# Folding a softmax into the first weight matrix with seven block products instead of eight, on a kernel bound by TensorE

## The chip, the cores and the metric

The kernel runs on one core of a Trainium2 chip. The metric is the device time of one execution in microseconds. Before the change it is 718.34 us, the median of 9 runs that lie between 718.19 and 718.52 us. A change of about 0.2% (1.4 us) is the least that a measurement here can tell from none.

## What is computed

The inputs are `q`, `k`, `v` of shape (4, 6080, 256), and two weight matrices `w_in` (256 x 2048) and `w_out` (2048 x 256), all fp32.

```python
# per batch b
qn = q / (norm(q, axis=1) + 1e-6);  kn = k / (norm(k, axis=1) + 1e-6)
a  = softmax(kn.T @ qn / tau)               # 256 x 256
x  = v @ a                                  # 6080 x 256
# over all 4 x 6080 tokens
g  = s * relu(x @ w_in) ** 2 + b
out = g @ w_out
```

The kernel never forms `x`. It folds the softmax into the weights: `v @ (a @ w_in)`, so that each batch has a folded matrix `wa = a @ w_in` (256 x 2048).

## The kernel before, in words

**Tiles and groups.** The tokens are taken in 48 groups of 512 (the last has 256). A group is worked in 16 steps, one for each 128 columns of `wa`. In step `m`, `mm1` (L661) makes two matmuls of 512 columns into one half of a PSUM tile `h_ps`; after two steps ScalarE takes the whole tile through a relu (L671). `h_ps` has two buffers. The squares of the relus are made on ScalarE after steps 3 and 5 (L682) and on VectorE after steps 8, 12 and 0 of the next group (L684).

**The second product, with seven.** For groups 1 to 46 `g @ w_out` is made by a Strassen-like scheme of seven block products in place of eight (`seven_items`, L829): 112 matmuls of 128 columns for a group, 7 in each step of the next group, one product finished every 16 matmuls. Its sums of `g` are made on VectorE (`sums_of`, after steps 2, 3, 6 and 10), and after each product VectorE scales it out of PSUM (`evacuate`, L689; called u or o_sb by what it writes).

**The order is written by hand.** The main loop runs over the steps. In each step it issues `mm1`, then any `early` function, then seven matmuls of the second product, then the relu, the squares and the sums, and at last the functions that stand for this step in `side`. `po` keeps the program order on each engine. So where a function stands in the step decides what is ahead of it in the queue of its engine.

**Batches.** While the groups of batch b are worked, the Gram matrix and the norms of batch b+1 are made on the side. Near the end of batch b `finish_ops` (placed by `fin_step` through the table `FIN`) takes the norms to inverse norms, scales, takes exponentials (`eT`, L302), sums their rows (L312) and their reciprocals (`rs`, L317), and then folds: `fold_one` makes a block of `wa`, 512 columns for one half m of the rows, from two matmuls of 512 columns that accumulate in PSUM (L329), and `scaled` writes it as fp16 times `rs`, on ScalarE for m = 0 (L322) and on VectorE for m = 1 (L324). For batches 1 to 3 there are 8 such blocks, three steps apart. All of them use one PSUM bank, the only buffer of the pool `ps_gram`, so a fold's first matmul waits until the block before it has been read. `wa` has two buffers (`apool`).

**The start.** Batch 0 has nothing to hide behind. Its last three chunks of `q` and `k` (one of four rows a partition, two of two) are treated alone: their squares are made as they land (L177, L171, L174), the first chunk's squares are folded once from four rows to two on VectorE (`half`, L222), for k and for q, and matmuls with a vector of ones sum them (`add_norms`, L246 for k, L250 for q). Then come the inverse norms (L271), the scaling (L296), the exponentials, a first folded block of 256 columns (`first_block`, L345), two more folds of the second 256 columns (`folds[:2]`, L329), and only then the main loop. The other folds of batch 0 stand in `early`, by the table `FOLDS`.

```python
FIN = (0, 3, 5, 7, 9, 11, 13, 17, 19, 22)
FOLDS = (1, 1, 3, 3, 5, 5, 8, 8)
for f in (first_block, *folds[:2]):
    f()
```

Of the kernel before, what the change touches and what calls it, by code (L numbers as in the profile page):

```python
# [9 lines left out]
FP16 = mybir.dt.float16  # L10
# [3 lines left out]
ALU = mybir.AluOpType  # L14
# [3 lines left out]
def kernel(  # L18
# [47 lines left out]
    wpool = pool("wpool", 1)  # L66
    qk_pool = pool("qk_pool", 8)
    sq_pool = pool("sq_pool", 2)
    late_pool = pool("late_pool", NLATE)
    f3_pool = pool("f3_pool", 13)  # L70
    sm_pool = pool("sm", 1)
    apool = pool("apool", 2)
# [3 lines left out]
    gpool = pool("gpool", 2)  # L76
    spool = pool("spool", 1)
    upool = pool("upool", 4)
    opool = pool("opool", 2)

    ps_gram = pool("ps_gram", 1, space=PSUM)
# [29 lines left out]
    class Gram:  # L111
# [45 lines left out]
        def norm_ops(self, c):  # L157

            qc, kc = self.tiles[c]
            _, np_, jc = self.chunks[c]  # L160
            st = {}

            at_end = self.b == 0 and c >= len(self.chunks) - NLATE

            def squares(a, js):
                def f():
                    if "sq" not in st:
                        st["sq"] = (late_pool if at_end else sq_pool).tile(
                            [P, 2, JC, C], FP16, tag="sq", name="sq")
# [12 lines left out]
            def fold(half, arrays, last):  # L182
                def f():
                    src = st["f", 2 * half] if 2 * half < jc else st["sq"]
                    if ("f", half) not in st:
                        if last:
                            t = f3_pool.tile([P, 2, 1, C], FP16, tag="f3", name="f3")
                        else:
                            t = sq_pool.tile([P, 2, half, C], FP16, tag=f"f{half}", name="f")
                        st["f", half] = t  # L190
                    po(nc.vector.tensor_add(  # L191
                        st["f", half][:np_, arrays], src[:np_, arrays, :half, :],
                        src[:np_, arrays, half : 2 * half, :]))
                    if last and c == 0:
                        self.first = st["f", half]
                    if last and (c == 0 or self.b > 0 and c == len(self.chunks) - 1):
                        for rows in self.rows:
                            rows.append((st["f", half], np_, 1))
                return f

            def into_first():

                dst, src = self.first[:np_], st["f", 1][:np_]
                if self.b == 0:
                    po(nc.vector.tensor_add(dst, dst, src))
# [10 lines left out]
            if at_end and jc == 2:  # L216
                return ops + [unfolded]
            if at_end:
                def half(a):
                    if "h" not in st:  # L220
                        st["h"] = sq_pool.tile([P, 2, 2, C], FP16, tag="f2", name="h")
                    po(nc.vector.tensor_add(st["h"][:np_, a], st["sq"][:np_, a, :2],  # L222
                                            st["sq"][:np_, a, 2:]))
                    self.rows[a].append((st["h"], np_, 2))
                return ops + [half]
            if jc == 8:
                ops += [fold(4, slice(0, 1), False), fold(4, slice(1, 2), False)]
            ops += [fold(2, slice(0, 2), False), fold(1, slice(0, 2), True)]
            return ops + [into_first] if 0 < c < len(self.chunks) - 1 else ops
# [24 lines left out]
        def finish_ops(self):  # L254
# [3 lines left out]
            def inverse(a=None):  # L258

                n = C + CH if a is None else (CH, C)[a]  # L260

                def part(i):
                    if i == 0:
                        st["r", a] = sm_pool.tile([P, n], FP32, tag=f"r{a}", name=f"r{a}")
                        if a is None:
                            st["r", 1], st["r", 0] = st["r", a][:, :C], st["r", a][:, C:]
                    r = st["r", a]
                    func, kw = [(AF.Ln, dict(bias=tiny)), (AF.Exp, dict(scale=0.5)),
                                (AF.Ln, dict(bias=eps)), (AF.Exp, dict(scale=-1.0))][i]
# [84 lines left out]
            def fold_one(f0, n, m):  # L354
                def f():
                    wa_ps = self.bank("wa_ps", CH, C).rearrange("p a c -> p (a c)")[:, :n]
                    fold_mm(f0, n, m, wa_ps)
                    scaled(f0, n, m, wa_ps)
                return f

            if self.b == 0:
                blocks = [(2 * P, 2 * P), (4 * P, 2 * P), (6 * P, 2 * P), (2 * NW, NW), (3 * NW, NW)]
            else:
                blocks = [(f0, NW) for f0 in range(0, Dff, NW)]
            folds = [fold_one(f0, n, m) for f0, n in blocks for m in range(CH)]
            if self.b == 0:
                return [norms(1), *inverse(1), norms(0), *inverse(0), lambda: scale(CH),
                        lambda: first_block(2 * P)] + folds
            return [copy_out, norms_both, *inverse(), scale, lambda: exps(0), lambda: exps(1),
                    sums] + folds  # L370

        def bank(self, name, a, b):

# [144 lines left out]
        f()  # L518
    transpose_v(0)
    keep_busy(1)  # L520
    for f in (first_block, *folds[:2]):
        f()


    acc = opool.tile([P, 4, C], FP32, tag="o_sb", name="acc")
# [38 lines left out]
        po(nc.scalar.copy(out=T[:, ts(i, 2), :], in_=w[:, 0, :, :P] if T is T2 else w[:, 0, :, P:]))  # L564


    side, early = {}, {}

    def at_step(s, f):
# [2 lines left out]

    FIN = (0, 3, 5, 7, 9, 11, 13, 17, 19, 22)
    first_group = [b * N // TG for b in range(B)]
    FOLDS = (1, 1, 3, 3, 5, 5, 8, 8)
    for i, f in enumerate(folds[2:]):
        early.setdefault(FOLDS[i], []).append(f)
    at_step(14, lambda: po(nc.vector.tensor_scalar_mul(
        out=s_out, in0=s_bc, scalar1=1.0 / (LAM * LAM))))
# [22 lines left out]
    for b in range(1, B):  # L602
        gr = grams[b]
        w0 = first_group[b - 1] * FT + (26 if b == 1 else 6)
        w1 = first_group[b] * FT - 3
        NCH = len(gr.chunks)
        fin_len = 54
        span = (w1 - fin_len) - w0 - 12
        n = NCH * JC
        for c in range(NCH):  # L610
            sc = w0 + span * c * JC / n
            at_step(max(3, sc - 16), lambda gr=gr, c=c: gr.load(c))
            if c == 0:
                at_step(sc, gr.start)
            for j in range(JC):
                at_step(w0 + span * (c * JC + j) / n, lambda gr=gr, c=c, j=j: gr.mm(c, j))

            def norm_step(gr=gr, c=c, sc=sc):
                ops = gr.norm_ops(c)
                for i, f in enumerate(ops):  # L620
                    at_step(int(sc) + 2 + 1 + i * 3, f)
            at_step(sc + 1, norm_step)

        def fin_step(gr=gr, s=w1 - fin_len):
            ops = gr.finish_ops()
            for i, f in enumerate(ops):
                at_step(int(s) + 1 + (FIN[i] if i < len(FIN) else FIN[-1] + 3 * (i - len(FIN) + 1)), f)
        at_step(w1 - fin_len - 12, fin_step)


# [292 lines left out]
```

## Time and profile before

| | |
|---|---|
| median of 9 runs | 718.34 us |
| the profiled execution | 718.34 us, of which the trace's span is 716.6 us |
| PE (TensorE) busy | 697.1 us, 7417 matmuls |
| VectorE (DVE) busy | 624.4 us, 878 instructions |
| ScalarE (ACT) busy | 544.8 us, 592 instructions |
| granted TensorE clock | 0.997 |
| fold matmuls (L329, 512 columns) | 56 |
| fold results scaled on ACT (L322, 512 columns) | 13, mean 683 ns |
| fold results scaled on DVE (L324, 512 columns) | 15, mean 744 ns |

The profiled execution took exactly the median, and 1.7 us of it lie outside the span. A busy PE means that matmuls follow one another; their recorded durations overlap, so durations are better read from start to start. In the lines of the trace a name like `wa_ps<-w_in,eT` says what an instruction writes and reads, `L329` is its line in the code, and a bracket at the end tells how long the engine was idle and which instruction ended it.

### The profile page before, as it was taken

The page shows a single profiled execution, that of the slowest core. Times are in us where ns is not written, and L with a number is a line of the kernel's source. Part 1 is how long each engine was busy: PE and PEld are TensorE (multiplying, and loading weights), DVE is VectorE, ACT ScalarE, POOL GpSimd, SP SyncE. Part 2 cuts the span into 40 slices and gives each one's busy share as a digit, 9 for nine tenths or more (in the row PEclk, how much of TensorE's full clock was granted, in tenths as well). Part 3 has the DMA queues.
Part 4 walks back from the last instruction along what each step waited for, and adds up shares of the span by engine and source line. Part 5 has one row for each costly group of instructions (what it writes and reads, how often), then busy time and mean ns, then how long its engine had stood idle before and what let it go on. Part 6 is the DMA issues. An engine that isn't in the chain of part 4 may idle for free.

```text
span 716.6 us, 17483 instructions
## 1 busy us (share of the span) xinstructions
PE 697.1 (97%) x7417; PEld 503.7 (70%) x7417; DVE 624.4 (87%) x878; ACT 544.8 (76%) x592; POOL 110.9 (15%) x189
## 2 busy tenths in 40 slices
PE   4699999999999999999999999999999999999998
PEld 2456777776677777777677777777668777777777
DVE  4889999988789989998889899998887888888886
ACT  5779877787777777778777778777877777777875
POOL 4532332102101222101010222110000000000000
PEclk9999999999999999999999999999999999999999
DMA  9999999635565978444663878943323333321202
GB/s 236 207 259 170 156 176 140 120 91 121 113 124 109 136 134 144 112 89 94 135 143 59 147 132 126 153 91 75 100 63 75 94 71 75 97 60 46 82 31 75
DMA packets 87454, 83.47 MB, mean 116 GB/s; under 512 B 56304, under 2 KB 62256, under 8 KB 87376
## 3 DMA queue, kind: packets, MB, share of 16 engines
q0 software_dynamic: 26608, 43.40, 38.3%
q1 hardware_dynamic: 60192, 37.64, 21.8%
q8 instruction: 58, 0.95, 0.6%
q10 hardware_dynamic: 576, 1.31, 0.5%
q14 instruction: 20, 0.16, 0.1%
HBM read 78.91 MB, written 24.90 MB: 145 GB/s over the span
## 4 chain that ended last, share of the span: by engine, by line
PE 92%; DMA 4%; DVE 2%; ACT 1%; issue 0%; DVEq 0%; ACTq 0%
PE h_ps L661 45%; PE o_ps L829 40%; PE s_ps L148 4%; PE wa_ps L329 2%; DMA qk<-in_k_dram 1%; DMA raw<-in_q_dram 1%; DMA w_in<-in_moe_w_in_dram 1%; PE o_ps L733 1%; ACT sq L177 1%; DVE f L191 1%; PE o_ps L707 0%; ACT r L671 0%; DVE sq L174 0%; DVE o_sb L689 0%; DVE S L758 0%
## 5 line engine op out<-in xcount | busy, mean ns | idle before, releaser
L671 ACT ACTIVATE r<-h_ps 128x1024 f16<-128x1024 f32 (+1 forms) x384 | 388.4, 1014 | 152.3 <-PE h_ps L661 147.6
L661 PE MATMUL h_ps<-vT,wa 128*128 128x512 f16 (+7 forms) x1632 | 452.1, 364 | 0.1
L829 PEld LDWEIGHTS <-S 128*128 128x128 f16 x2944 | 198.0, 98 | 84.8 <-issue 0.2
L829 PEld LDWEIGHTS <-g 128*128 128x128 f16 x2208 | 155.1, 98 | 74.1
L684 DVE TENSOR_TENSOR g<-r 128x2048 f16<-128x2048 f16 (+2 forms) x150 | 174.7, 1165 | 14.0 <-ACT r L671 13.4
L829 PE MATMUL o_ps<-T,S 128*128 128x128 f16 x2208 | 183.3, 219 | 0.1
L661 PEld LDWEIGHTS <-wa 128*128 128x128 f16 x1632 | 136.0, 98 | 20.1 <-DVE wa L324 0.5
L829 PE MATMUL o_ps<-w_out,g 128*128 128x128 f16 x1472 | 134.3, 219 | 0.2 <-DVE u L689 0.2
L689 DVE SCALAR_TENSOR_TENSOR o_sb<-o_ps,s_out,u 128x256 f32<-128x256 f32 x138 | 66.5, 482 | 50.8 <-PE o_ps L829 48.7
L682 ACT ACTIVATE g<-r 128x1024 f16<-128x1024 f16 (+1 forms) x97 | 100.4, 1035 | 0.2
L148 PE MATMUL s_ps<-qk 128*128 128x256 f16 (+1 forms) x384 | 72.0, 290 | 13.5 <-ACT qk L139 9.0
L388 POOL DMA_DIRECT2D v<-in_v_dram x48 | 30.9, 648 | 264.8 <-DMA vT<-v 209.7
L689 DVE SCALAR_TENSOR_TENSOR u<-o_ps,s_out,rowconst 128x256 f32<-128x256 f32 x138 | 65.8, 477 | 0.0
L829 PE MATMUL o_ps<-w_out,S 128*128 128x128 f16 x736 | 63.5, 219 | 0.0
L829 PE MATMUL o_ps<-N,g 128*128 128x128 f16 x736 | 63.4, 219 | 0.0
L207 POOL DMA_DIRECT2D f<-f x30 | 26.3, 876 | 223.8 <-DVE f L191 187.4
L758 DVE TENSOR_TENSOR S<-S,g 128x2048 f16<-128x2048 f16 (+1 forms) x47 | 56.4, 1201 | 1.3
L177 ACT ACTIVATE sq<-qk 128x1024 f16<-128x1024 f16 (+2 forms) x53 | 54.5, 1041 | 3.9 <-DMA qk<-in_k_dram 2.2
L756 DVE TENSOR_TENSOR S<-g 128x2048 f16<-128x2048 f16 (+1 forms) x47 | 56.1, 1193 | 0.0
L762 DVE TENSOR_TENSOR S<-g,S 128x2048 f16<-128x2048 f16 x46 | 55.9, 1216 | 0.0
L760 DVE TENSOR_TENSOR S<-g 128x2048 f16<-128x2048 f16 x46 | 55.9, 1215 | 0.0
L148 PEld LDWEIGHTS <-qk 128*128 128x128 f16 (+1 forms) x384 | 33.1, 104 | 20.5 <-ACT qk L139 9.5
(85 smaller groups left out, 314.0 us busy)
## 6 DMA issues: line engine op xcount, KB each, us to landing
out_dram<-o_sb SPq DMA_DIRECT2D x42, 512.0 KB, 2.9
v<-in_v_dram POOLq DMA_DIRECT2D x47, 256.0 KB, 4.9
qk<-in_k_dram POOLq DMA_DIRECT2D x42, 256.0 KB, 6.8
qk<-in_q_dram POOLq DMA_DIRECT2D x42, 256.0 KB, 7.6
f<-f POOLq DMA_DIRECT2D x30, 128.0 KB, 3.1
vT<-v SPq DMA_TRANSPOSE x182, 3.0
out_dram<-o_sb SPq DMA_DIRECT2D x10, 256.0 KB, 4.1
w<-in_moe_w_out_dram POOLq DMA_DIRECT2D x4, 512.0 KB, 10.1
```

The source lines that it names most:

```text
L148: po(nc.tensor.matmul(self.s_ps[:, ch, :], qc[:np_, j, ts(ch, P)], kc[:np_, j, :], start=(c == 0 and j == 0 and ch == 0), stop=(c == len(s ...
L177: po(nc.scalar.activation(out=st["sq"][:np_, a, js, :], in_=(qc, kc)[a][:np_, js, :], func=AF.Square))
L661: po(nc.tensor.matmul(dst, wa[:, ci, ts(m, P)], src, start=(ci == 0), stop=(ci == CH - 1), skip_group_check=True))
L671: po(nc.scalar.activation(out=r16[:, :, i % 2, :n], in_=h_tiles.pop((g, i))[:, :, :n], func=AF.Relu))
L682: po(nc.scalar.activation(out=dst, in_=src, func=AF.Square))
L684: po(nc.vector.tensor_mul(dst, src, src))
L689: po(nc.vector.scalar_tensor_tensor(out=dst, in0=src, scalar=s_out, op0=ALU.mult, in1=add, op1=ALU.add))
L756: po(nc.vector.tensor_add(T[1], A21, A22))
L758: po(nc.vector.tensor_sub(T[2], T[1], A11))
L760: po(nc.vector.tensor_sub(T[3], A11, A21))
L762: po(nc.vector.tensor_sub(T[4], A12, T[2]))
L829: po(nc.tensor.matmul(st[name][:, j, :], a()[:, i, ts(j, P)], w[:, i, :], start=first, stop=last, skip_group_check=True))
```

## The change

There are three parts.

1. **Start.** The two folds of the second 256 columns are no longer made ahead of the main loop, but in its step 0, after the first two `mm1` matmuls.
2. **Start.** Of the first of the last three chunks, only the squares of k are folded from four rows to two. The rows of q's squares are summed as they are: 8 small matmuls in place of a VectorE addition and 4.
3. **Folds of batches 1 to 3.** The 8 blocks of two matmuls are replaced by seven products for each half of the columns, 14 matmuls of 512 columns in all. They need sums of the halves of `eT` (`half_sums`, four VectorE operations of 128 columns for a batch) and of the halves of `w_in` (`w_in_sums`, four VectorE operations of 1024 columns, once, kept in the buffers of the last chunks' squares). Partial results are accumulated on in the same bank: after each product the bank is read, and the next product is added to what stands there (`new` marks the three of seven that begin afresh). Three of seven readings are kept as fp32 (`keep`, ScalarE), one goes to `wa` by ScalarE and three by VectorE with a kept one added (`out`). The products stand 2.4 steps apart, rounded down, in place of 3.

The diff, cut to its core:

```diff
-    late_pool = pool("late_pool", NLATE)
+    late_pool = pool("late_pool", 1)
+    fold_pool = pool("fold_pool", 1)
...
             if at_end:
-                def half(a):
-                    if "h" not in st:
-                        st["h"] = sq_pool.tile([P, 2, 2, C], FP16, tag="f2", name="h")
-                    po(nc.vector.tensor_add(st["h"][:np_, a], st["sq"][:np_, a, :2],
-                                            st["sq"][:np_, a, 2:]))
-                    self.rows[a].append((st["h"], np_, 2))
-                return ops + [half]
+                def rows(a):
+                    if a == 0 or jc == 2:
+                        return unfolded(a)
+                    half = sq_pool.tile([P, 2, 2, C], FP16, tag="f2", name="half")
+                    po(nc.vector.tensor_add(half[:np_, 1], st["sq"][:np_, 1, :2], st["sq"][:np_, 1, 2:]))
+                    self.rows[1].append((half, np_, 2))
+                return ops + [rows]
...
+            def half_sums():
+                A = lambda m, k: st["e"][:, k, ts(m, P)]
+                S = st["S"] = [fold_pool.tile([P, P], FP16, tag=f"S{n}", name=f"S{n}")
+                               for n in range(1, 5)]
+                po(nc.vector.tensor_add(S[0], A(1, 0), A(1, 1)))
+                po(nc.vector.tensor_sub(S[1], S[0], A(0, 0)))
+                po(nc.vector.tensor_sub(S[2], A(0, 0), A(1, 0)))
+                po(nc.vector.tensor_sub(S[3], A(0, 1), S[1]))
+
+            def seven_folds(p):
+                A = lambda m, k: st["e"][:, k, ts(m, P)]
+                B = lambda k, n: w_in16[:, k, ds(n * (Dff // 2) + p * NW, NW)]
+                T = lambda n: W[n][:, ts(p, NW)]
+                S = lambda n: st["S"][n - 1]
+                C_ = lambda m, n: self.wa[:, m, ds(n * (Dff // 2) + p * NW, NW)]
+                rs = lambda m: st["rs"][:, m : m + 1]
+                u = {}
+                def product(a, w, then, new=False):
+                    def f():
+                        if new:
+                            st["wa_ps"] = self.bank("wa_ps", CH, C).rearrange("p a c -> p (a c)")
+                        po(nc.tensor.matmul(st["wa_ps"], a(), w(), start=new, stop=True,
+                                            skip_group_check=True))
+                        then()
+                    return f
+                def keep(n, m):
+                    def f():
+                        u[n] = fold_pool.tile([P, NW], FP32, tag=f"u{n}", name=f"u{n}")
+                        po(nc.scalar.mul(out=u[n], in_=st["wa_ps"], mul=rs(m)))
+                    return f
+                def out(m, n, k=None):
+                    def f():
+                        if k is None:
+                            po(nc.scalar.mul(out=C_(m, n), in_=st["wa_ps"], mul=rs(m)))
+                        else:
+                            po(nc.vector.scalar_tensor_tensor(
+                                out=C_(m, n), in0=st["wa_ps"], scalar=rs(m), op0=ALU.mult,
+                                in1=u[k], op1=ALU.add))
+                    return f
+                return [
+                    product(lambda: A(0, 0), lambda: B(0, 0), keep(1, 0), True),
+                    product(lambda: S(2), lambda: T("T2"), keep(2, 0)),
+                    product(lambda: S(3), lambda: T("T3"), keep(3, 1)),
+                    product(lambda: A(1, 1), lambda: T("N4"), out(1, 0)),
+                    product(lambda: A(0, 1), lambda: B(1, 0), out(0, 0, 1), True),
+                    product(lambda: S(1), lambda: T("T1"), out(1, 1, 3), True),
+                    product(lambda: S(4), lambda: B(1, 1), out(0, 1, 2)),
+                ]
...
-            else:
-                blocks = [(f0, NW) for f0 in range(0, Dff, NW)]
...
+            def sums_and_halves():
+                sums()
+                half_sums()
+
             return [copy_out, norms_both, *inverse(), scale, lambda: exps(0), lambda: exps(1),
-                    sums] + folds
+                    sums_and_halves] + seven_folds(0) + seven_folds(1)
...
-    for f in (first_block, *folds[:2]):
-        f()
+    first_block()
...
+    def w_in_sums(i):
+        F = Dff // 2
+        B = lambda k, n: w_in16[:, k, ds(n * F, F)]
+        if i == 0:
+            c0, c1, c2 = range(NCH0 - NLATE, NCH0)
+            W["T1"] = late_pool.tile([P, F], FP16, tag=f"sq{c1}", name="T1w")
+            W["T2"] = late_pool.tile([P, F], FP16, tag=f"sq{c2}", name="T2w")
+            both = late_pool.tile([P, 2, F], FP16, tag=f"sq{c0}", name="TNw")
+            W["T3"], W["N4"] = both[:, 0], both[:, 1]
+        po([lambda: nc.vector.tensor_sub(W["T1"], B(0, 1), B(0, 0)),
+            lambda: nc.vector.tensor_sub(W["T2"], B(1, 1), W["T1"]),
+            lambda: nc.vector.tensor_sub(W["T3"], B(1, 1), B(0, 1)),
+            lambda: nc.vector.tensor_sub(W["N4"], B(1, 0), W["T2"])][i]())
...
-    FOLDS = (1, 1, 3, 3, 5, 5, 8, 8)
-    for i, f in enumerate(folds[2:]):
+    FOLDS = (0, 0, 1, 1, 3, 3, 5, 5, 8, 8)
+    for i, f in enumerate(folds):
         early.setdefault(FOLDS[i], []).append(f)
...
         def fin_step(gr=gr, s=w1 - fin_len):
+            if gr.b == 1:
+                for i in range(4):
+                    at_step(int(s) + 4 + 4 * i, lambda i=i: w_in_sums(i))
             ops = gr.finish_ops()
             for i, f in enumerate(ops):
-                at_step(int(s) + 1 + (FIN[i] if i < len(FIN) else FIN[-1] + 3 * (i - len(FIN) + 1)), f)
+                at_step(int(s) + 1 + (FIN[i] if i < len(FIN) else FIN[-1] + 2.4 * (i - len(FIN) + 1)), f)
```

More of the change, by code (lines that the diff above doesn't have):

```diff
@@ L167, in f @@
                     if "sq" not in st:
-                        st["sq"] = (late_pool if at_end else sq_pool).tile(
-                            [P, 2, JC, C], FP16, tag="sq", name="sq")
+                        if at_end:
+                            st["sq"] = late_pool.tile([P, 2, jc, C], FP16, tag=f"sq{c}", name="sq")
+                        else:
+                            st["sq"] = sq_pool.tile([P, 2, JC, C], FP16, tag="sq", name="sq")
                     if a == 1 and at_end and c == len(self.chunks) - 1:
@@ L215, in norm_ops @@
                 ops += [squares(1, js), squares(0, js)]
-            if at_end and jc == 2:
-                return ops + [unfolded]
             if at_end:
-                def half(a):
-                    if "h" not in st:
-                        st["h"] = sq_pool.tile([P, 2, 2, C], FP16, tag="f2", name="h")
-                    po(nc.vector.tensor_add(st["h"][:np_, a], st["sq"][:np_, a, :2],
-                                            st["sq"][:np_, a, 2:]))
-                    self.rows[a].append((st["h"], np_, 2))
-                return ops + [half]
+                def rows(a):
[5 more added lines that the diff above has]
+                return ops + [rows]
             if jc == 8:
@@ new lines, in seven_folds @@
+            def seven_folds(p):
[23 more added lines that the diff above has]
+                            po(nc.scalar.mul(out=C_(m, n), in_=st["wa_ps"], mul=rs(m)))
+                        else:
+                            po(nc.vector.scalar_tensor_tensor(
[11 more added lines that the diff above has]
+                ]
@@ L361, in finish_ops @@
             if self.b == 0:
                 blocks = [(2 * P, 2 * P), (4 * P, 2 * P), (6 * P, 2 * P), (2 * NW, NW), (3 * NW, NW)]
-            else:
-                blocks = [(f0, NW) for f0 in range(0, Dff, NW)]
-            folds = [fold_one(f0, n, m) for f0, n in blocks for m in range(CH)]
-            if self.b == 0:
+                folds = [fold_one(f0, n, m) for f0, n in blocks for m in range(CH)]
                 return [norms(1), *inverse(1), norms(0), *inverse(0), lambda: scale(CH),
@@ L564, in cast_w @@
         po(nc.scalar.copy(out=T[:, ts(i, 2), :], in_=w[:, 0, :, :P] if T is T2 else w[:, 0, :, P:]))
+    W = {}
+    def w_in_sums(i):
[11 more added lines that the diff above has]
+            lambda: nc.vector.tensor_sub(W["N4"], B(1, 0), W["T2"])][i]())
     side, early = {}, {}
```

## The prediction

> **What bounds the kernel now.** I read four views in this order. First the page's busy times and the chain that ended last:
>
> ```profile
> PE 697.1 (97%) x7417; PEld 503.7 (70%) x7417; DVE 624.4 (87%) x878; ACT 544.8 (76%) x592; POOL 110.9 (15%) x189
> ...
> PE 92%; DMA 4%; DVE 2%; ACT 1%; issue 0%; DVEq 0%; ACTq 0%
> ```
>
> TensorE is busy 97% of the span and makes 92% of the chain. Busy is not yet saturated, so I looked at what PE waited for, over the whole span:
>
> ```profile
> PE s_ps L148 <- ACT qk L139: 9.0, 2, 7.1
> PE s_ps L148 <- DMA qk<-in_q_dram: 4.4, 4, 1.3
> PE n_ps L246 <- DVE h L222: 1.3, 1, 1.3
> PE wa_ps L329 <- DMA w_in<-in_moe_w_in_dram: 0.5, 1, 0.5
> PE r_ps L340 <- ACT eT L302: 0.5, 1, 0.5
> PE o_ps L829 <- DVE u L689: 0.2, 1, 0.2
> ```
>
> All but the last belong to the start. From about 38 us on PE streams almost without a hole, so a matmul removed there is time gained in full, and a wait put there is time lost in full: nothing later gives it back. What is left to ask is whether the new folds make PE wait. For that the timeline of ScalarE where the folds of batch 2 stand (steps 2 to 7 of a group):
>
> ```profile
> 341.75 1.02 ACT L671 ACTIVATE r<-h_ps 128x1024 f16<-128x1024 f32 x1 [0.47 <-PE h_ps L661]
> ...
> 342.67 1.05 ACT L682 ACTIVATE g<-r 128x1024 f16<-128x1024 f16 x1
> ...
> 343.82 1.02 ACT L671 ACTIVATE r<-h_ps 128x1024 f16<-128x1024 f32 x1
> ...
> 344.74 1.05 ACT L682 ACTIVATE g<-r 128x1024 f16<-128x1024 f16 x1
> ...
> 345.66 0.59 PE L329 MATMUL wa_ps<-w_in,eT 128*128 128x512 f16 x2
> 345.69 1.02 ACT L671 ACTIVATE r<-h_ps 128x1024 f16<-128x1024 f32 x1
> ...
> 346.59 0.69 ACT L322 ACTIVATE wa<-wa_ps,rs 128x512 f16<-128x512 f32 x1
> ```
>
> Here ACT has no idle time: relu, square, relu, square, relu, fold result, one behind the other. ACT's 76% is a mean; around steps 3 to 7 of a group it is full. And the start of the dense part:
>
> ```profile
> 37.40 0.61 PE L329 MATMUL wa_ps<-w_in,eT 128*128 128x256 f16 x4 [0.54 <-DMA w_in<-in_moe_w_in_dram]
> 37.85 0.59 PE L661 MATMUL h_ps<-vT,wa 128*128 128x512 f16 x2
> ```
>
> The two early folds wait for the second piece of w_in, and the first h matmuls wait behind them.
>
> **What the Trainium skill says.** (1) TensorE: Matmul & The Clock Gate, "Back-to-back issue gap": an isolated matmul follows the one before after N/2.4 + 2.5 ns, 216 ns for 512 columns; it also gives 131 ns as sustained. The trace agrees with the first: in the chain pairs of L661 take 0.43 us. (2) The same page, in its section on the array, says that ScalarE and VectorE are strict first-in first-out and that matmuls stay in program order. The trace agrees: the fold result of 346.59 stands behind a relu, and only follows when that is through. (3) PSUM — Partial Sum Buffer, "The four PSUM rules": a partial sum may be read in the middle of an accumulation group if the read is synchronised. The change lives on this; the synchronisation is a wait of the next product for the reader. No run yet shows it in this kernel.
>
> **The change part by part.**
>
> *Matmuls removed.* Three batches go from 16 matmuls of 512 columns to 14: 6 x 0.216 = 1.30 us less on a saturated PE. Weight loads go along, hidden (PEld 70%).
>
> *Waits added.* The eight old blocks stood three steps apart. The 14 products stand at floor(2.4 n) steps, and by the table that puts them after steps 0, 2, 5, 7, 10, 12, 14 of one group and 1, 3, 6, 8, 10, 13, 15 of the next (the same for each batch). All use one bank, so product n+1 waits until the reading of product n is done, and behind it wait PE's next h matmuls and everything else of PE, which is in order. Durations, start to start, from the timeline: a step without folds 0.82 us (L661 pairs at 346.09, 346.91, 347.73); a product 0.22; on ACT a relu 0.92 (341.75 to 342.67), a square 0.95 (344.74 to 345.69), a fold result 0.57 (186.28 to 186.84 in batch 1), and 0.68 until it has ended; on DVE an o_sb 0.40 (350.50 to 350.90), a 2048-element operation 1.14 (346.74 to 347.88), a fold result 0.66 (344.11 to 344.77), and 0.75 until it has ended. A result can be read 0.41 us after its matmul's start (L661 pair at 339.04, relu at 339.67, less 0.22). From an engine's end to a waiting matmul I take 0.05 us (exponential ended 36.37, L340 at 36.42). The fp32 output and the third operand of the new readings are not shown for ACT; I take the same 0.68 (an fp32 result of 258 columns from PSUM, L271, takes 0.47 as an fp16 one of 256, L322, does), and for DVE 0.75 (L689 with 512 columns: 0.74).
> - Product 3 to 4, reader ACT. In ACT's program order between the readings of products 2 and 3 stand relu, square, relu, square. From the start of product 2: 0.41 + 0.57 + 0.92 + 0.95 + 0.92 + 0.95 + 0.68 + 0.05 = 5.45. PE is ready for product 4 after 0.22 + 3 x 0.82 + 0.22 + 2 x 0.82 = 4.54. Wait 0.91.
> - Product 6 to 7, reader DVE, behind an o_sb and a square. From the start of step 12: o_sb starts at 0.69 (349.81 to 350.50), + 0.40 + 1.14 + 0.75 + 0.05 = 3.03; PE ready at 0.82 + 0.22 + 1.64 = 2.68. Wait 0.35.
> - Product 10 to 11, ACT. From step 3: relu at 0.63, then 0.92 + 0.95 + 0.57 + 0.92 + 0.95 + 0.68 + 0.05 = 5.67; PE: 0.82 + 0.22 + 2.46 + 0.22 + 1.64 = 5.36. Wait 0.31.
> - Product 13 to 14, DVE, late because its square waited for that last relu: 12.26 against 12.07 from the same step. Wait 0.19.
> - The other gaps close with 0.1 to 1.5 us to spare by the same sums.
>
> A batch waits 1.76 us, three batches 5.28. Bounds: at least the first wait alone, 0.91 x 3 = 2.7, if DVE and the later relus are quicker than I have them; at most some 0.9 more a batch, 8.0, if every reading is a fifth slower and a late relu then holds a buffer of h_ps. I take 5.28.
>
> *Work added on ACT and DVE.* A batch has 4 more results on ACT and 2 more on DVE; what they cost is in the waits above. The four half sums (128 columns, SBUF) aren't in the trace; VectorE: DVE Perf Modes, "The TRN2 errata", gives 58 + N/2 cycles at 0.96 GHz, 0.13 us, and its single-operation fixed term of about 150 gives 0.22: 0.5 to 0.9 us in all, an estimate. They stand behind the reciprocal at 337.72, where DVE is idle for 1.25 us before 339.13. Nothing. The four sums of w_in cost 0.69 each (L191, 1024 elements), once, in steps 11, 15, 3, 7 before batch 1's folds. DVE has holes of 1.25 us there, and the o_sb behind them have about half a microsecond until PE needs their bank: nothing; up to 0.3 if they bunch up.
>
> *Start.* The q addition (0.42 us, L222) goes and 4 small matmuls (0.03 us apart) come. PE waited for that addition from about 33.16 to 33.40; it now runs through, and q's norms end about 0.11 earlier, and with them the exponentials and the first block. The first h matmuls need only that block (its first columns were ready at 37.28), not the w_in piece that landed at 37.35; the moved folds find it landed. So the dense part begins at about 37.2 in place of 37.40. Gain 0.15, between 0 (if a relu or w_in is late next) and 0.25. No DMA is issued elsewhere, and the order on the queues of POOL and SP stays as it was.
>
> *Sum.* -1.30 + 5.28 - 0.15 = +3.83. The span goes from 716.6 to 720.4; 1.7 us lie outside it. That execution took just the median, so 718.34 + 3.83 = 722.2 us.
>
> **The rivals.** *A, only the first wait is real:* what speaks for it is that the other three are differences of long sums, 0.19 to 0.35; against, that they come from the same durations. 3 x 0.91 - 1.30 - 0.15 = +1.3: 719.6. *B, no waits, a gain:* the other side. One mechanism: ACT catches up before product 4. It decides at the square and relu pair: if ACT needed less than 4.54 us from product 2 to the end of reading 3, or if a step in this stretch took over 1.0 us, PE would not wait. 718.34 - 1.30 - 0.15 = 716.9. Against it stands that ACT has no idle time in that stretch and its order there is fixed. *C, the waits spread:* late relus keep h_ps buffers, PE waits at L661 too, and DVE's readings come later; +0.9 a batch: 725. For it: after product 11 the relu of step 7 ends only 0.2 us before PE needs its buffer. Against: each wait gives ACT and DVE time to catch up.
>
> **How the numbers follow.** Forecast 722.2 with 0.70, A 0.12, B 0.08, C 0.10. The range goes from A's 719.6 to 724.2, which leaves out B and most of C. A change under 0.2% (1.4 us) can't be told from none. Faster by more than that, below 716.9: half of B and little else, 0.05. Within: the rest of B and half of A, 0.09. Slower: 0.86.
>
> **What would show it.** PE waits for ACT at the line of `product`, one of about 0.9 us and one of 0.3 in each batch, and for DVE two of 0.2 to 0.35; the h matmuls' first start near 37.2; 7415 matmuls. If PE shows no waits there, my order of ACT or the step length is wrong. If it waits at L661's successor, C.

## The result, and the profile after

The changed kernel takes 722.48 us, the median of 9 runs (722.34 to 722.91), against 718.39 for the kernel before, measured beside it: a ratio of 1.0058, 95% interval 1.0049 to 1.0066. It is 4.1 us slower. The forecast was 722.2 us. The span of the profiled execution went from 716.6 to 720.8 us.

The busy times and the chain that ended last, from the page of the changed kernel:

```profile
PE 696.0 (97%) x7415; PEld 502.4 (70%) x7415; DVE 632.6 (88%) x899; ACT 551.0 (76%) x604; POOL 110.8 (15%) x189
...
PE 87%; ACT 6%; DVE 3%; DMA 3%; issue 1%; ACTq 0%; DVEq 0%
```

PE is busy 1.1 us less and the span is 4.2 us longer, so PE now stands still for some 5 us more. ScalarE's part of the chain, 1% before, is 6%: where PE waits for ScalarE, the chain leaves PE and runs back through ScalarE's full queue, which is more than the wait itself. The waits of PE, summed over the span (engine, line, what it waited for: us in all, times, the longest), but for two rows of the start (L149, which was L148) that are over before the dense part begins:

```profile
...
PE wa_ps L386 <- ACT u L394: 2.2, 3, 0.7
PE n_ps L247 <- DVE half L224: 1.3, 1, 1.3
PE wa_ps L386 <- DVE wa L402: 0.5, 3, 0.2
PE h_ps L738 <- ACT wa L323: 0.5, 1, 0.5
PE o_ps L906 <- DVE u L766: 0.4, 2, 0.2
PE r_ps L341 <- ACT eT L303: 0.3, 1, 0.3
```

L386 is the matmul of `product`, L394 the reading of `keep`, L402 the reading of `out` on VectorE. The two rows of L386 are new, and so is one of the two waits at L906 (the second product, which waits for its evacuation, L766). The row of L738 stands in place of the fold's wait for `w_in` at the start. This view understates a wait, because it counts from the end of the matmul before, and a matmul of 128 columns is recorded with 0.22 us though the next follows after 0.06. So I also took start to start: for each matmul after 40 us, the time to the next start less what its N columns take (N/2.4 + 2.5 ns, the formula of the prediction; in this trace matmuls of 512, 256 and 128 columns follow one another after 0.216, 0.109 and 0.056 us). Summed, these holes are 3.1 us before and 8.7 us after. The holes over 0.1 us that only the changed kernel has:

```
hole (us) ahead of     batch 1   batch 2   batch 3
product 4              0.906     0.905     0.905
product 7              0.336     0.336     0.338
product 11             0.299     0.298     0.298
product 14             0.145     0.146     0.144
a batch                1.69      1.69      1.69
L906, at 158.9 us      0.185
L906, at 161.0 us      0.375
```

The products' holes are the same in every batch, 5.06 us in all; the two at L906 stand in batch 0's groups, where the sums of `w_in` are made, 0.56 us in all. With the six matmuls removed: 5.06 + 0.56 - 1.30 = 4.3 us; the span grew by 4.2 and the median by 4.1. (In an in-order stream the time is work plus holes, so this says where the time went; why the holes are there is for the experiments.)

The place of the largest hole, batch 2, from the timeline of the changed kernel (start us, duration us, engine, line, what; in the bracket the idle time before it and what ended it):

```profile
342.66 0.38 PE L386 MATMUL wa_ps<-T2w,S 128*128 128x512 f16 x1
...
343.08 0.69 ACT L394 ACTIVATE u<-wa_ps,rs 128x512 f32<-128x512 f32 x1 [0.26 <-PE wa_ps L386]
...
343.66 1.02 ACT L748 ACTIVATE r<-h_ps 128x1024 f16<-128x1024 f32 x1
...
344.57 1.06 ACT L759 ACTIVATE g<-r 128x1024 f16<-128x1024 f16 x1
345.34 0.38 PE L386 MATMUL wa_ps<-TNw,S 128*128 128x512 f16 x1
345.51 1.02 ACT L748 ACTIVATE r<-h_ps 128x1024 f16<-128x1024 f32 x1
...
346.42 1.06 ACT L759 ACTIVATE g<-r 128x1024 f16<-128x1024 f16 x1
...
347.36 0.70 ACT L394 ACTIVATE u<-wa_ps,rs 128x512 f32<-128x512 f32 x1
...
348.11 0.38 PE L386 MATMUL wa_ps<-TNw,eT 128*128 128x512 f16 x1 [0.74 <-ACT u L394]
```

Product 3 is made at 345.34, but its reading stands in ACT's queue behind a relu and a square and begins only at 347.36. It ends at 348.06, and product 4 starts 0.05 us later. From product 2 to product 4 it is 348.11 - 342.66 = 5.45 us, the figure of the prediction.

The start, in the same view:

```profile
36.94 0.62 ACT L323 ACTIVATE wa<-wa_ps,rs 128x128 f16<-128x128 f32 x2 [0.56 <-PE wa_ps L346]
...
37.36 0.61 PE L738 MATMUL h_ps<-vT,wa 128*128 128x512 f16 x2 [0.48 <-ACT wa L323]
...
37.80 0.38 PE L330 MATMUL wa_ps<-w_in,eT 128*128 128x256 f16 x2
```

The h matmuls no longer wait for a fold that waits for `w_in`: they follow the first block, and the fold comes after them. But they begin at 37.36, where the dense part began at 37.40 before.

### The profile page after: what moved, and what is told of

The parts are those of the page before. It is cut to its first block, busy times and chain, and to the rows that moved or that the text cites. A ratio compares the mean times of both kernels' runs of the same rounds, so it can differ in the third digit from the quotient of the medians.

```text
span 720.8 us, 17509 instructions
## 1 busy us (share of the span) xinstructions
PE 696.0 (97%) x7415; PEld 502.4 (70%) x7415; DVE 632.6 (88%) x899; ACT 551.0 (76%) x604; POOL 110.8 (15%) x189
## 4 chain that ended last, share of the span: by engine, by line
PE 87%; ACT 6%; DVE 3%; DMA 3%; issue 1%; ACTq 0%; DVEq 0%
PE h_ps L738 42%; PE o_ps L906 37%; PE s_ps L149 4%; ACT g L759 2%; ACT r L748 2%; DMA qk<-in_k_dram 1%; DMA raw<-in_q_dram 1%; PE wa_ps L386 1%; ACT u L394 1%; ACT sq L180 1%; PE o_ps L810 1%; DVE f L194 1%; PE o_ps L784 0%; DVE o_sb L766 0%; PE wa_ps L330 0%
## 5 line engine op out<-in xcount | busy, mean ns | idle before, releaser
L738 PE MATMUL h_ps<-vT,wa 128*128 128x512 f16 (+7 forms) x1632 | 452.3, 364 | 0.6 <-ACT wa L323 0.5
L906 PEld LDWEIGHTS <-S 128*128 128x128 f16 x2944 | 198.0, 98 | 85.0 <-issue 0.2
L906 PEld LDWEIGHTS <-g 128*128 128x128 f16 x2208 | 155.0, 98 | 74.1
L906 PE MATMUL o_ps<-T,S 128*128 128x128 f16 x2208 | 183.5, 219 | 0.1
L738 PEld LDWEIGHTS <-wa 128*128 128x128 f16 x1632 | 136.4, 98 | 25.0 <-issue 5.7
L906 PE MATMUL o_ps<-w_out,g 128*128 128x128 f16 x1472 | 134.2, 219 | 0.4 <-DVE u L766 0.4
L766 DVE SCALAR_TENSOR_TENSOR o_sb<-o_ps,s_out,u 128x256 f32<-128x256 f32 x138 | 66.3, 481 | 38.4 <-PE o_ps L906 36.3
L149 PE MATMUL s_ps<-qk 128*128 128x256 f16 (+1 forms) x384 | 70.2, 283 | 15.8 <-ACT qk L140 9.2
L766 DVE SCALAR_TENSOR_TENSOR u<-o_ps,s_out,rowconst 128x256 f32<-128x256 f32 x138 | 65.9, 478 | 0.0
L906 PE MATMUL o_ps<-w_out,S 128*128 128x128 f16 x736 | 63.5, 219 | 0.0
L906 PE MATMUL o_ps<-N,g 128*128 128x128 f16 x736 | 63.4, 219 | 0.0
L149 PEld LDWEIGHTS <-qk 128*128 128x128 f16 (+1 forms) x384 | 32.2, 101 | 21.7 <-ACT qk L140 9.7
```

The lines of the kernel that those rows point to most:

```text
L149: po(nc.tensor.matmul(self.s_ps[:, ch, :], qc[:np_, j, ts(ch, P)], kc[:np_, j, :], start=(c == 0 and j == 0 and ch == 0), stop=(c == len(s ...
L738: po(nc.tensor.matmul(dst, wa[:, ci, ts(m, P)], src, start=(ci == 0), stop=(ci == CH - 1), skip_group_check=True))
L766: po(nc.vector.scalar_tensor_tensor(out=dst, in0=src, scalar=s_out, op0=ALU.mult, in1=add, op1=ALU.add))
L906: po(nc.tensor.matmul(st[name][:, j, :], a()[:, i, ts(j, P)], w[:, i, :], start=first, stop=last, skip_group_check=True))
```

## The experiments

The theory: all of the loss is holes in PE's stream at places where the one-bank partial sum is read late, plus two where the sums of `w_in` delay VectorE; what is saved is six matmuls. The rivals: the start edits carry a part of it; the matmuls removed weren't worth their 1.30 us; or the folds cost something that no table of steps can take away. Each run is given with the median of the kernel before that was measured beside it.

**1. The folds alone.** The start as before, the rest as changed:

```
-    first_block()
+    for f in (first_block, *folds[:2]):
+        f()
...
-                    if a == 0 or jc == 2:
+                    if jc == 2:
```

> The folded batches as in the changed kernel, with the two edits of the start undone. My theory (the start edits move nothing that can be measured, the five holes per batch and the two of the w_in sums make all of it): 722.4 to 722.5, the same as the changed kernel. Rival (the start edits cost or gain a part when they stand with the folds): off that by 0.15 us or more, to either side.

(This undoes both edits of the start: k's and q's squares are both folded again, and the table of the early folds is that of before. The expectation speaks of five holes a batch; there are four.) Measured: 722.62 us against 718.41, ratio 1.0059 (1.0046 to 1.0071), with the same four holes a batch and the same two at the second product. The folds make the whole loss.

**2. The start alone.** The changed kernel with eight folds a batch, three steps apart, as before, and without the sums of `w_in`:

```
-            return [... sums_and_halves] + seven_folds(0) + seven_folds(1)
+            return [... sums] + [fold_one(f0, NW, m) for f0 in range(0, Dff, NW) for m in range(CH)]
```

> The kernel before with only the two start edits (q's rows summed unfolded, second folded block behind the first tile). Theory as predicted: 0.15 us less, 718.2, with the first h matmul near 37.2. Rival (the profile after: loads landed 0.2 us later, the first h matmul was at 37.36): nothing, 718.4. If the late loads belong to the change, they are seen here too.

Measured: 718.36 us against 718.29, ratio 1.0000 (0.9992 to 1.0008). The start edits do nothing that can be measured here; a gain of 0.15 us, which the theory forecast, would not be seen in this interval either, so the run does not tell the theory from its rival. In the nine profiles with the new start the dense part begins between 37.12 and 37.78 us, with 37.21 in the middle; in the three with the old start at 37.36, 37.40 and 37.63. The gain may be there, but one execution scatters by more than it.

**3. What six matmuls are worth.** The kernel before, with the first 512 columns of `wa` of batches 1 to 3 made from half the rows of `w_in` (so the other half is left out):

```
-                for j in range(CH):
+                nj = 1 if self.b > 0 and f0 == 0 else CH
+                for j in range(nj):
```

> The kernel before with six matmuls of 512 columns left out: in batches 1 to 3 the first 512 columns of the folded matrix are made from half of the rows of w_in alone, so two matmuls a batch and their part of the sum are missing. Nothing else moves. Theory: 6 x 0.216 = 1.30 us less, 717.1. Rival (PE has slack in these stretches or gives it back elsewhere): less than half of it.

Measured: 717.07 us against 718.35, ratio 0.9982 (0.9975 to 0.9989): 1.28 us, 0.213 for each. That is beside the 0.216 that the prediction took: the saving is real and, as far as the interval tells, whole.

**4. The sums of `w_in` alone.** Run 2 with the four sums made where the change makes them, and used by nothing:

```
+            if gr.b == 1:
+                for i in range(4):
+                    at_step(int(s) + 4 + 4 * i, lambda i=i: w_in_sums(i))
```

> The start-only run with the four sums of w_in added at the steps where the changed kernel has them, made but not used; the folds are the old eight blocks. Theory: PE waits 0.19 and 0.37 us near 159 and 161 us as in the changed kernel, 0.56 us more than the start-only run, 718.9. Rival (the waits come from the fold's other new work): no difference.

Measured: 718.71 us against 718.35, ratio 1.0006 (0.9998 to 1.0015). The interval alone doesn't tell this from nothing; the trace does, for it has the same two holes, 0.18 and 0.37 us, which run 2 has not. VectorE's queue there, in the changed kernel, with PE's waiting matmul:

```profile
157.72 0.68 DVE L638 TENSOR_TENSOR TNw<-w_in 128x1024 f16<-128x1024 f16 x1
...
158.33 0.48 DVE L766 SCALAR_TENSOR_TENSOR u<-o_ps,s_out,rowconst 128x256 f32<-128x256 f32 x1
...
158.72 0.68 DVE L297 TENSOR_TENSOR sm_t<-sm_t,rNone 128x512 f32<-128x512 f32 x1
...
159.32 1.22 DVE L837 TENSOR_TENSOR S<-g 128x2048 f16<-128x2048 f16 x1
...
160.46 0.48 DVE L766 SCALAR_TENSOR_TENSOR u<-o_ps,s_out,rowconst 128x256 f32<-128x256 f32 x1
160.85 0.68 DVE L639 TENSOR_TENSOR TNw<-w_in,T2w 128x1024 f16<-128x1024 f16 x1
...
160.99 0.22 PE L906 MATMUL o_ps<-w_out,g 128*128 128x128 f16 x1 [0.21 <-DVE u L766]
```

The sum of L638, the third of the four, puts off everything behind it by 0.61 us (157.72 to 158.33), and behind it comes, besides the evacuations, the scaling of the softmax (L297), another 0.60. PE lost 0.56 of the 0.61: the second evacuation had 0.05 us to spare. Both holes come from this one sum; the fourth (L639) starts only behind the second evacuation, and no hole of over 0.1 us follows it.

**5. Product 3 one step earlier.** The first table that I tried for the products; only product 3 of each batch is moved (its counterpart in the second half, product 10, stays), so that its reading stands ahead of the second relu and square:

```
-    FIN = (0, 3, 5, 7, 9, 11, 13, 17, 19, 22)
+    FIN = (0, 3, 5, 7, 9, 11, 13, 17, 19, 22,
+           24, 26, 28, 31, 34, 36, 38, 41, 43, 46, 48, 50, 53, 55)
...
-                at_step(int(s) + 1 + (FIN[i] if i < len(FIN) else FIN[-1] + 2.4 * (i - len(FIN) + 1)), f)
+                at_step(int(s) + 1 + FIN[i], f)
```

> The changed kernel with the third and the tenth product one step or none earlier: only product 3 moves, from step 5 to step 4, so that ScalarE reads it before, not behind, the relu and the square of step 5; products 4 to 14 stay. Theory (the wait is ScalarE's queue ahead of the reader): product 4 no longer waits, three times 0.91 us less, 719.8 us; the waits at products 7, 11 and 14 stay as they are, 0.34, 0.30 and 0.15 a batch. Rival (two steps are too short for one bank, whatever is queued): product 3, now two steps behind product 2, waits in its place, and the time stays near 722.4.

Measured: 722.14 us against 718.29, ratio 1.0054 (1.0041 to 1.0067). A miss: the hole of product 4 is gone, and product 6 now waits 0.72 us, which it did not before. The time is the rival's, but not its mechanism: product 3, two steps behind product 2, does not wait. From the timeline of this kernel, the same batch:

```profile
340.54 0.38 PE L386 MATMUL wa_ps<-w_in,eT 128*128 128x512 f16 x1
...
345.25 0.69 ACT L394 ACTIVATE u<-wa_ps,rs 128x512 f32<-128x512 f32 x1
...
346.94 0.38 PE L386 MATMUL wa_ps<-TNw,eT 128*128 128x512 f16 x1
...
347.67 1.04 ACT L749 ACTIVATE r<-h_ps 128x1024 f16<-128x1024 f32 x1
...
348.75 1.23 DVE L762 TENSOR_TENSOR g<-r 128x2048 f16<-128x2048 f16 x1 [1.28 <-ACT r L749]
...
351.41 0.75 DVE L402 SCALAR_TENSOR_TENSOR wa<-wa_ps,rs,u 128x512 f16<-128x512 f32 x1
...
352.21 0.38 PE L386 MATMUL wa_ps<-T1w,S 128*128 128x512 f16 x1 [0.56 <-DVE wa L402]
```

and from that of the changed kernel:

```profile
340.80 0.38 PE L386 MATMUL wa_ps<-w_in,eT 128*128 128x512 f16 x1
...
347.93 1.04 ACT L748 ACTIVATE r<-h_ps 128x1024 f16<-128x1024 f32 x1
...
351.67 0.75 DVE L402 SCALAR_TENSOR_TENSOR wa<-wa_ps,rs,u 128x512 f16<-128x512 f32 x1
```

Product 1 stands at 340.54 here and at 340.80 in the changed kernel. Counted from there, product 4 comes at 6.40 us in place of 7.31: PE has its 0.91 us. But the relu of 347.67 (347.93 in the changed kernel) starts at 7.13 us in both kernels, and the reading of product 5 on VectorE (L402, 351.67 in the changed kernel) at 10.87 us in both. ACT had the same work in another order and was full from the reading of product 2 until then; VectorE stood idle 1.28 us for its relu, so its square and the reading behind it were no earlier. PE only arrived sooner at the next reading that was not yet done. I had summed a single wait and not carried the gain to the next reading.

**6. Another table, and the sums of `w_in` moved.** Two runs. The second differs from the first only in the sums:

```
+           24, 26, 28, 31, 33, 35, 37, 40, 42, 44, 47, 49, 51, 53)
...
-                    at_step(int(s) + 4 + 4 * i, lambda i=i: w_in_sums(i))
+                    at_step(int(s) + (7, 7, 23, 26)[i], lambda i=i: w_in_sums(i))
```

> The changed kernel with its 14 products at steps chosen by hand, 0, 2, 4, 7, 9, 11, 13 of each of the two groups, so that each reader stands ahead of the squares and not behind them. Same instructions, same bank, two-step gaps in plenty. Theory: by the same sums no product waits; 5.06 us less than the changed kernel, 717.4 us, and PE shows no wait at the line of product. What then remains against the kernel before is -1.3 for six matmuls and +0.56 for the w_in sums. Rival (one bank with fewer than three steps between products must wait): at least the product after each ScalarE reading waits on, and the time stays above 719.

> As the run with the hand-made table, and the four sums of w_in moved from steps where VectorE is full into its holes (two after step 14 of the group before last, one after step 14 of the last, one after step 1 of the next). Theory (the 0.56 us that PE waited near 159 and 161 us come from the sums' crowding the readings of the second product): these waits go, 716.9 us, 0.2% under the kernel before. Rival (they come from something else in that stretch, a DMA or the norms): they stay, 717.4.

Measured: 720.74 us, ratio 1.0033 (1.0020 to 1.0046), and 720.18 us, ratio 1.0026 (1.0016 to 1.0036), both against 718.29. The first is a miss: no wait was expected, and two a batch are left. Products 5 and 12 wait 0.535 us each, now for ACT's reading of products 4 and 11 (L400); from the waits of the first of the two:

```profile
PE wa_ps L386 <- ACT wa L400: 2.2, 6, 0.4
...
PE o_ps L907 <- DVE u L767: 0.4, 2, 0.2
```

My sum had let a relu ahead of that reading start when its data came, though ACT was still behind. A recurrence over the queues, in which each instruction starts at the later of its data and the end of the one ahead, gives 0.54 us for these holes and 0.73 for product 6 in run 5 (0.72 in the trace); I made it after these misses, so what it forecast is runs 7 and 8. Moving the sums took both holes at L906 away. The medians differ by 0.56 us, just their size, though each is known less closely than that; counted from the first matmul of the dense part, the two profiled spans differ by 0.54.

**7. Product 3 read on VectorE.** The change with one reading moved to the other engine:

```
-                        po(nc.scalar.mul(out=u[n], in_=st["wa_ps"], mul=rs(m)))
+                        if n == 3:
+                            po(nc.vector.tensor_scalar_mul(out=u[n], in0=st["wa_ps"], scalar1=rs(m)))
+                        else:
+                            po(nc.scalar.mul(out=u[n], in_=st["wa_ps"], mul=rs(m)))
```

> The changed kernel with its own steps, where the reading of the third product of each half (kept as fp32) is made by VectorE in place of ScalarE. Distances between the products, bank and PE's order are the same. Theory (ScalarE's queue ahead of the reading): the waits of product 4 (0.91) and product 11 (0.30) go, product 14's with the latter; VectorE's readings come a little later, product 6 waits 0.16 and product 7 stays at 0.34; 0.50 in place of 1.69 a batch, 718.9 us. Rival (distance in steps): waits at products 4 and 11 stay, 722.4.

Measured: 718.83 us against 718.35, ratio 1.0008 (1.0000 to 1.0016). Products 3 and 4 of batch 2, with VectorE's reading between them:

```profile
343.91 0.38 PE L386 MATMUL wa_ps<-TNw,S 128*128 128x512 f16 x1
...
344.61 0.74 DVE L395 TENSOR_SCALAR u<-wa_ps,rs 128x512 f32<-128x512 f32 x1
...
345.77 0.38 PE L386 MATMUL wa_ps<-TNw,eT 128*128 128x512 f16 x1
```

The reading has ended 0.42 us before product 4 starts. The holes of products 4, 11 and 14 are gone, 6 has 0.145 and 7 has 0.328, as the recurrence had it. Two instructions a batch on the other queue take away 3.6 of the 4.1 us, with the products at the same steps: the cause of these three holes is ScalarE's queue, not the distance of the products. Product 7's stays, since its reading was on VectorE all along, behind an evacuation and a square.

**8. A table without waits.** Each reading placed where its engine has room by the recurrence (the edits are those of run 6, with another second line of the table):

```
+           23, 25, 31, 33, 35, 37, 39, 41, 44, 48, 50, 53, 55, 57)
...
+                    at_step(int(s) + (7, 7, 23, 26)[i], lambda i=i: w_in_sums(i))
```

> The changed kernel with the w_in sums in VectorE's holes, and the 14 products at steps -1, 1, 7, 9, 11, 13, 15, 17, 20, 24, 26, 29, 31, 33 of the last two groups: none between steps 2 and 6 of the first, where ScalarE is full. Theory: the same queue sums that give the waits of the two tables already run (product 6 waits 0.73 in one, products 5 and 12 wait 0.54 in the other) leave 0.03 us a batch here; against the run with the sums moved, 3.2 us less, 717.0 us, 0.2% under the kernel before. Rival (a reading between two products costs PE something even where nobody waits, or another wait takes its place as it did twice): 718 or more, with waits at the product or at the h matmuls.

Measured: 717.34 us against 718.35, ratio 0.9986 (0.9980 to 0.9993). One hole is left that was not expected, 0.32 us ahead of product 1 of batch 1, which needs the bank that the row sums were read from:

```profile
164.81 0.68 DVE L638 TENSOR_TENSOR TNw<-w_in 128x1024 f16<-128x1024 f16 x1
165.41 0.17 DVE L318 RECIPROCAL rs<-r_ps 128x2 f32<-128x2 f32 x1
...
165.63 0.38 PE L386 MATMUL wa_ps<-w_in,eT 128*128 128x512 f16 x1 [0.16 <-DVE rs L318]
```

**9. The same, with that sum one step later.** `(7, 7, 24, 26)` in place of `(7, 7, 23, 26)`:

> The table of no_waits with the w_in sum of the third table entry one step later, behind the step in which VectorE sums the rows that product 1 of batch 1 waits for. My theory (a wait of TensorE lasts as long as VectorE's queue puts the row sum off): the 0.32 us wait of product 1 in batch 1 goes, 717.34 - 0.32 = 717.0. Rival (the row sum is late by its own data, not by the queue ahead of it): the wait stays and so does 717.3.

Measured: 717.05 us against 718.41, ratio 0.9983 (0.9976 to 0.9989). The same queue now:

```profile
164.88 0.16 DVE L318 RECIPROCAL rs<-r_ps 128x2 f32<-128x2 f32 x1
...
165.37 0.38 PE L386 MATMUL wa_ps<-w_in,eT 128*128 128x512 f16 x1
...
165.61 0.68 DVE L638 TENSOR_TENSOR TNw<-w_in 128x1024 f16<-128x1024 f16 x1
```

No hole of over 0.1 us is left that the kernel before doesn't have, though most products stand only two steps apart, and the gain is the six matmuls: 1.36 us, beside 1.28 in run 3. This version beats both kernels, the one before by 0.17%, with an interval that lies clear of 1, though it is a little under the 1.4 us named at the outset as the least to be told from none.

Holes of the trace and medians together, in us, each less that of the kernel before. "Dense part" is the profiled span counted from the first matmul of the dense part (679.16 us before), so that the scatter of the start is out of it; "median" is the measured difference:

```
kernel               products  w_in sums  matmuls   sum    dense part  median
the change             5.06      0.56      -1.30    4.32      4.28       4.09
folds alone            5.06      0.56      -1.30    4.32      4.27       4.21
start alone            0         0          0       0         0.00       0.07
six fewer              0         0         -1.30   -1.30     -1.23      -1.28
w_in sums alone        0         0.56       0       0.56      0.54       0.36
product 3 earlier      4.49      0.56      -1.30    3.75      3.72       3.85
other table            3.21      0.56      -1.30    2.47      2.46       2.45
and sums moved         3.21      0         -1.30    1.91      1.91       1.89
reading on VectorE     1.42      0.56      -1.30    0.68      0.67       0.48
no waits               0.32      0         -1.30   -0.98     -0.89      -1.01
no waits, second       0         0         -1.30   -1.30     -1.22      -1.36
```

The sums agree with the dense part within 0.09 us, as they nearly must where PE works in order, and with the medians, which no trace enters, within 0.25 us; no further cost is seen at that size. The table alone does not show the cause. That is done by the runs in which the queue ahead of a reading was changed and the hole went with it: 7 at the products' own steps, 6 for the sums of `w_in`, and 9, whose 0.32 us went with one sum that was moved by one step.

## Why the prediction was right, point by point

- *What bounds the kernel.* Right. PE is saturated after 38 us; a matmul taken out there came back in full (run 3), and a hole put there was lost in full (the sums and the dense part of the table). Two readings were a little off. In the stretch of before that the prediction shows, ScalarE has 0.10 us to spare at 343.72, ahead of the second relu, besides the 0.47 ahead of the first. It is full in the changed kernel because the reading of product 2 (343.08) was put there, which the sum did count. And the fold result at 346.59 starts 0.12 us before the recorded end of the relu ahead of it (345.69 and 1.02 us long): the trace shows the order on ScalarE, and that one starts 0.9 us behind the other, not that it waits for the recorded end.
- *Matmuls removed, -1.30.* Right, 1.28 measured alone.
- *Waits added, 1.76 a batch.* Right in place, reader and nearly in size: 0.91, 0.35, 0.31, 0.19 forecast, 0.91, 0.34, 0.30, 0.15 measured, 5.06 in all in place of 5.28. The three later ones are small differences of long sums and still held to 0.05 us: the instructions that the sum of product 11 counts follow one another on ScalarE without a hole (from the relu at 359.20 to the reading at 363.49), and those of products 7 and 14 on VectorE (from 352.52 and from 365.13), in the order that the prediction had. The estimate of 0.05 us from a reader's end to the waiting matmul is what the trace shows (348.06 to 348.11). So is the reading's length, for which I took that of the fp16 result: 0.69 us with the fp32 one.
- *Half sums, nothing.* Right. No hole of over 0.1 us follows them on PE in any batch. In batch 2 the evacuation behind them still waited for PE:

```profile
340.08 0.22 DVE L370 TENSOR_TENSOR S<-eT,S 128x128 f16<-128x128 f16 x1
...
340.89 0.48 DVE L766 SCALAR_TENSOR_TENSOR o_sb<-o_ps,s_out,u 128x256 f32<-128x256 f32 x1 [0.59 <-PE o_ps L906]
```

- *Sums of w_in, "nothing; up to 0.3 if they bunch up".* This term was mis-sized: 0.56 us. I had counted on VectorE's holes of 1.25 us and on half a microsecond that the evacuations had to spare. The first two sums found room, and no hole follows them. The third, in step 3, fell into a stretch in which VectorE was already working without a hole and also scales the softmax (L297), which the prediction did not count; there 0.05 us was to spare, and this one sum made both holes. It was not that the sums bunched up.
- *Start, -0.15.* The mechanism came (the h matmuls go ahead of the fold), the size can't be confirmed: 0.04 us in this profile (37.40 to 37.36), 0.07 us the other way in the medians of run 2, 0.12 us in the measured differences of run 1 and the change. The middle of the nine starts is 0.19 us ahead of the middle of the three old ones, but the medians do not show it: they lie 0.07 us under the dense part in the mean of the nine kernels with the new start, and 0.06 in the two runs with the old one. It lies in the forecast bounds of 0 to 0.25 and below what the runs resolve, and stays open.
- *Rivals.* A (only the first wait): all four are there. B (no waits): wrong for this table; run 9 reaches its 717 us, but with other steps, not because ScalarE caught up. C (waits spread to L738): no new wait at L738. But a form of C that I hadn't priced came in the experiments: take one wait away and the next reading waits.

In the trace the waits came out 0.22 below the forecast, the sums of `w_in` 0.56 and the start 0.11 above, which makes 4.3 of the forecast 3.8; the median came out 0.3 us above the predicted time. That it is so close is partly luck: the waits, forecast too long, made up for a third of what the other two terms missed.

## What to carry to other kernels

Count a saving on a saturated in-order engine against every wait that comes with it: here 14 readings of one PSUM bank, a batch, two or three steps of 0.82 us apart, cost four times what the six matmuls brought (5.06 us against 1.30). Work out such waits as a recurrence over the queues, each instruction starting at the later of its data and the end of the one ahead, and carry it past the first wait, since a gain ahead of a full engine only moves the wait. Then look for the steps in which the reader has room, or give one reading to the other engine, before giving the idea up.

## What the runs showed that I had not expected

- Moving one product by one step took 0.91 us of waiting a batch away from product 4, put 0.72 ahead of product 6, and gave back only 0.57 us of the holes of three batches; in the medians it is 0.34 (722.48 to 722.14), which their intervals don't tell from nothing.
- A 128-column sum of two fp16 tiles of 128 partitions takes VectorE 0.20 to 0.23 us, with 0.14 from one start to the next in the two that don't wait for the one ahead (339.80, 339.94, 340.08). The Trainium skill, VectorE: DVE Perf Modes, "The TRN2 errata", is where the prediction's estimates of 0.13 and 0.22 us come from: here the first is near the pitch from start to start, the second near the duration.
- The reading in the middle of a sum, which the Trainium skill allows when it is synchronised (PSUM — Partial Sum Buffer, "The four PSUM rules"), costs no more than the reading of a finished sum did before: 0.69 us at 343.08, between products 2 and 3 that add to the same tile, and 0.69 at 346.59 in the kernel before. What it costs is the order that it forces: the next product waits for the reading.
